# The first 512 rows: weights of three blocks per transfer, ScalarE's copy ahead of the next root, the next tile's turn between up products

## The chip, the cores and the metric

The kernel runs on one core of one Trainium2 chip. The metric is the device time of one execution in microseconds (us), the median over several runs. The engines of the core work side by side, each through its own list of instructions in order: TensorE (PE) multiplies matrices, VectorE (DVE) and ScalarE (ACT) do elementwise work, GpSimd (POOL) helps, and SyncE (SP) issues most of the transfers from the large memory. They wait for each other through semaphores.

## What is computed

The input x has 2048 rows of 640 columns. It is normalised row by row, and the result xn goes through two parts: an attention part of 32 heads (keys and values of the last 512 positions), and a gated part with weights of 640 x 1536. The two are multiplied at the end.

```python
def _B_ref(x, w_gate, w_up, w_down):
    g = jnp.einsum("bsd,df->bsf", x, w_gate)
    u = jnp.einsum("bsd,df->bsf", x, w_up)
    h = _sigmoid(g) * u
    return jnp.einsum("bsf,fd->bsd", h, w_down)

x = A_x
xn = _layernorm(x, axis=-1)
s = _A_ref(xn, A_k_cache, A_v_cache, A_wq, A_wo)
g = _silu(_B_ref(xn, B_w_gate, B_w_up, B_w_down))
return x + s * g
```

The change lies in the first two products of `_B_ref` and in the normalisation, for the first 512 rows alone.

## The kernel before

The 2048 rows are four groups of 512, and a group is four tiles of 128 rows. The 1536 columns of `w_gate` and `w_up` are 12 blocks of 128, the 640 columns of x five chunks of 128. For a group, the loop over the blocks (`for f in range(NF)`) makes ten matmuls per block, five chunks for the gate and five for the up product, each 128 x 128 weights against 512 rows (L487). ACT takes the sigmoid of the gate (L492), DVE multiplies it with the up product into `hT_sb` (L493). The results of a block lie in two banks of PSUM, and four such pairs (`bank2`) are used in turn.

These matmuls need xn turned, so that its columns lie on the partitions. Groups 1 to 3 are turned by a transposing transfer. Group 0 has nothing to hide behind, so its tiles are handled one by one, in the order written out in the loop `for q in range(TQ)`, and the first three blocks (FA = 3) are multiplied tile by tile as each becomes ready:

- `ln_part`, `ln_stats` (L357, L362): DVE's statistics of a tile, in two parts of 320 columns, and their sum.
- `ln_sqrt` (L401): ACT's square root. The reciprocal (L418) and `ln_apply` (L372) on DVE give the tile of xn; that of tile 0 comes in two pieces.
- `turn` (L408): PE transposes the five chunks of the tile into one of two PSUM banks, and ACT copies them (L410) into `xnT[0]`, which stands as `mid` in the profile.
- `first_mm(q, f)` (L395): ten matmuls of 128 x 128 weights against the 128 rows of tile q, the five chunks of the gate and then the five of the up product of block f.
- `warm_up` (L385): products of zeros that keep PE busy, nine ahead of everything and two behind the turn of tile 0.

In this order a tile is turned one or two blocks ahead of the products that use it. Tile 1 is turned behind block 0 of tile 0, and block 1 of tile 0 comes behind it; block 2 of tiles 0 and 1 is put off until tile 2 is turned, block 2 of tile 2 until tile 3 is turned. On ACT the root of tile q + 1 stands ahead of the copy of tile q.

All loads of the first rows are issued from SP's queue in the written order: x tiles 0 and 1, then gate and up weights in pieces given by `f_cuts` (three pieces of one block, then three of three blocks), with x tiles 2 and 3 behind the first two pairs of pieces, and the x of group 1 behind the fourth pair. `load_w` (L330) issues one piece, `load_x` (L309) one tile of x, `load_x4` (L314) four. From the ninth transfer on, an issue also waits for the landing of the one eight places ahead of it. Behind the weights follow four loads of `wq` for a scan (L201).

Of the kernel before, what the change touches and what calls it, by code (L numbers as in the profile page):

```python
# [17 lines left out]
def kernel(  # L18
# [14 lines left out]
    P = 128  # L33
# [7 lines left out]
    F = B_w_gate.shape[1]  # L41
# [8 lines left out]
    TQ = 4  # L50
    NCD = D // P
# [4 lines left out]
    G = 2  # L56
    NG = NPAIR // G
    assert NG == 8 and HQDH == 48 * P and NST == 4
    NWARM = (9, 2)
    FA = 3  # L60
    PC = 3
    GC = 2 * G * DH
# [212 lines left out]
    with ExitStack() as bctx:  # L275
# [31 lines left out]
        def load_x(t):  # L307
            x_sb = xin_pool.tile([P, D], BF16, name=f"x_sb{t}")
            nc.sync.dma_start(x_sb[:], xf[t * P:(t + 1) * P, :])  # L309
            x_tiles[t] = x_sb[:]  # L310

        def load_x4(s):
            x_sb = xin_pool.tile([P, TQ, D], BF16, name="x_sb4")
            nc.sync.dma_start(  # L314
                x_sb[:], xf[s * 512:(s + 1) * 512, :].rearrange("(q p) d -> p q d", p=P)
            )
            for q in range(TQ):
                x_tiles[s * TQ + q] = x_sb[:, q, :]

        wg_sb = wB.tile([P, NCD, F], BF16, name="wg_sb")  # L320
        wu_sb = wB.tile([P, NCD, F], BF16, name="wu_sb")
        wg_r = B_w_gate.rearrange("(c p) f -> p c f", p=P)
        wu_r = B_w_up.rearrange("(c p) f -> p c f", p=P)
        f_cuts = [0, P, 2 * P, 3 * P, 6 * P]
        while f_cuts[-1] < F:
            f_cuts.append(min(F, f_cuts[-1] + 3 * P))

        def load_w(w_sb, w_r, k):
            f = slice(f_cuts[k], f_cuts[k + 1])
            nc.sync.dma_start(w_sb[:, :, f], w_r[:, :, f])  # L330
# [3 lines left out]
        for k in range(len(f_cuts) - 1):  # L334
            load_w(wg_sb, wg_r, k)
            load_w(wu_sb, wu_r, k)
            if k < 2:
                load_x(2 + k)
            elif k == 3:
                load_x4(1)  # L340
        wd_sb = wB.tile([P, NF, D], BF16, name="wd_sb")
        for i in range(4):
# [11 lines left out]
        def ln_part(t, i):  # L354
            if i == 0:
                stats_t[t] = bwork.tile([P, nsub, nc.vector.BN_STATS_DIM], F32, name="stats")
            nc.vector.bn_stats(stats_t[t][:, i, :], x_tiles[t][:, i * fsz:(i + 1) * fsz])  # L357

        def ln_stats(t, i0=0):
            for i in range(i0, nsub):  # L360
                ln_part(t, i)
            nc.vector.bn_aggr(mv[:, t, :], stats_t[t][:])  # L362
# [5 lines left out]
        def ln_apply(t):  # L368
            xn = xpool.tile([P, D], BF16, name="xn")
            cuts = [0, 2 * P, D] if t == 0 else [0, D]  # L370
            for d in map(slice, cuts, cuts[1:]):
                nc.vector.tensor_scalar(  # L372
                    xn[:, d], x_tiles[t][:, d], mv[:, t, 0:1], rstd[:, t, :],
                    op0=ALU.subtract, op1=ALU.mult,
                )
            return xn
# [6 lines left out]
        def warm_up(n):  # L383
            for _ in range(n):
                nc.tensor.matmul(w_ps, lhsT=warm[:, 0:P], rhs=warm[:], start=True, stop=True)  # L385

        warm_up(NWARM[0])

        gu_first = [bank2() for _ in range(FA)]

        def first_mm(q, f):
            r = slice(q * P, (q + 1) * P)
            for i, w in enumerate((wg_sb, wu_sb)):
                for c in range(NCD):
                    nc.tensor.matmul(  # L395
                        gu_first[f][:, i, r], lhsT=w[:, c, f * P:(f + 1) * P], rhs=xnT[0][:, c, r],
                        start=(c == 0), stop=(c == NCD - 1),
                    )

        def ln_sqrt(q):  # L400
            nc.scalar.activation(  # L401
                rstd[:, q:q + 1, :], mv[:, q:q + 1, 1:2], AF.Sqrt, bias=eps_t[:], scale=1.0
            )

        def turn(q):
            pT = pT_banks[:, q % 2, 0:NCD * P // 2].bitcast(BF16).rearrange("p (c n) -> p c n", c=NCD)
            for c in range(NCD):
                nc.tensor.transpose(pT[:, c, :], xn_t[q][:, c * P:(c + 1) * P], ident[:])  # L408
            for cs in ((slice(0, 2), slice(2, NCD)) if q == 0 else (slice(0, NCD),)):
                nc.scalar.activation(xnT[0][:, cs, q * P:(q + 1) * P], pT[:, cs, :], AF.Copy)  # L410

        xn_t = {}
        ln_stats(0)
        ln_sqrt(0)
        for q in range(TQ):
            if q + 1 < TQ:
                ln_part(q + 1, 0)
            nc.vector.reciprocal(rstd[:, q:q + 1, :], rstd[:, q:q + 1, :])  # L418
            xn_t[q] = ln_apply(q)
            if q + 1 < TQ:  # L420
                ln_stats(q + 1, 1)
                ln_sqrt(q + 1)
            if q == 0:
                turn(0)
                warm_up(NWARM[1])
                continue
            first_mm(q - 1, 0)
            turn(q)
            first_mm(q - 1, 1)
            if q == 2:  # L430
                first_mm(0, 2)
                first_mm(1, 2)
            elif q == 3:
                first_mm(2, 2)
        for f in range(FA):
            first_mm(TQ - 1, f)

        def ln_rest(t):
            xn = ln_apply(t)
# [483 lines left out]
    for r, (pi, g) in enumerate(runs):  # L923
# [23 lines left out]
        for k, (q, x) in enumerate(pv_list):  # L947
# [5 lines left out]
            if pi == 0 and 1 <= g < 5 and k == 6:  # L953
                w = wo_in[3 * g % 4]
# [260 lines left out]
```

## Time and profile before

| | us |
|---|---|
| median of 3 runs | 872.84 (872.71 to 873.98) |
| the profiled execution, whole | 873.17 |
| its span, first to last instruction | 871.4 |
| PE busy | 864.6 |
| DVE busy | 674.6 |
| ACT busy | 625.5 |
| POOL busy | 212.4 |

The span is that of one profiled execution; its whole time has 1.8 us more, around the span. The first rows end where the loop of L487 begins, near 15 us. In the timeline a row has its start, the time from the first start to the last end of the instructions merged in it, engine, line, operation, output <- inputs, how many there are, and in square brackets how long the engine stood idle before it and what released it. The end of a matmul is modelled: back to back, matmuls of 128 columns start every 0.056 us, but each is shown as 0.22 us long. In the chain of waits a row has a start, a length and what ran; "issue" is time in which nothing shown was waited for. A row of transfers has the form, how many, KB, and the median time from issue to landing.

### The profile page before, as it was taken

To read this page: it belongs to the slowest core of one execution; us is meant where nothing else is said; L and a number is where in the kernel's file an instruction comes from. 1 tells how busy PE (TensorE), PEld (TensorE's weight loads), DVE (VectorE), ACT (ScalarE), POOL (GpSimd) and SP (SyncE) were. 2 spreads that over 40 slices of the span, in tenths; PEclk is the share of its full clock that TensorE was granted. 3 is DMA by queue.
4 is the path that set the end of the run, shared out by engine and by line. 5 is a ranking of instruction groups with operands and counts; after the bars stand their busy time and mean duration, and the time that the engine had idled before them with its cause. 6 is when DMAs were issued, how large, how long until landed. Compare 5 with 4: busy or idle time off the path is not lost.

```text
span 871.4 us, 18973 instructions
## 1 busy us (share of the span) xinstructions
PE 864.6 (99%) x7558; PEld 565.2 (65%) x7569; DVE 674.6 (77%) x1137; ACT 625.5 (72%) x772; POOL 212.4 (24%) x299
## 2 busy tenths in 40 slices
PE   8999999999999999999999999999999999999998
PEld 5444455756766756756756756756777777777776
DVE  6587777777777777777677777787878587989997
ACT  6868676488888788788788787774655667666662
POOL 0000239406406406406406406300000111000000
PEclk9999999999999999999999999999999999999999
DMA  9999982699699799699689779497788788465841
GB/s 273 273 273 223 269 178 56 88 240 197 136 251 195 153 235 190 146 246 183 153 223 170 165 180 215 111 293 203 202 208 231 249 277 279 146 226 203 283 161 38
DMA packets 264712, 174.69 MB, mean 200 GB/s; under 512 B 162256, under 2 KB 249680, under 8 KB 264624
## 3 DMA queue, kind: packets, MB, share of 16 engines
q1 hardware_dynamic: 258192, 153.23, 69.3%
q0 software_dynamic: 6432, 20.26, 11.6%
q8 instruction: 59, 0.97, 0.5%
q14 instruction: 29, 0.24, 0.1%
HBM read 102.11 MB, written 35.13 MB: 157 GB/s over the span
## 4 chain that ended last, share of the span: by engine, by line
PE 96%; DVE 2%; ACT 1%; issue 1%; DMA 0%; ACTq 0%; DVEq 0%
PE ps_all L1022 24%; PE ps_all L606 21%; PE ps_all L714 20%; PE ps_all L700 19%; PE ps_all L487 9%; PE ps_all L560 1%; PE ps_all L395 1%; ACT sig_sb L492 1%; ACT mid L244 0%; DVE stats L357 0%; DVE arm L1006 0%; DMA x_sb<-in_A_x_dram 0%; DVE hT_sb L493 0%; DVE arm L1077 0%; DVE arm L1075 0%
## 5 line engine op out<-in xcount | busy, mean ns | idle before, releaser
L704 ACT ACTIVATE E<-ps_all 128x1024 bf16<-128x1024 f32 x256 | 251.2, 1022 | 113.5 <-PE ps_all L700 112.8
L700 PE MATMUL ps_all<-qT,kT 64*128 64x512 bf16 x1536 | 198.2, 376 | 0.0
L714 PEld LDWEIGHTS <-E 128*128 128x128 bf16 x2048 | 169.7, 98 | 8.1 <-issue 8.1
L714 PE MATMUL ps_all<-v_sb,E 128*128 128x193 bf16 x2048 | 174.0, 247 | 0.0
L644 DVE TENSOR_TENSOR qT<-ps_all,qp 128x512 bf16<-128x512 f32 x174 | 115.5, 687 | 47.4 <-PE ps_all L606 38.6
L1022 PEld LDWEIGHTS <-mid 128*128 128x128 f16 x1176 | 115.0, 98 | 44.6
L700 PEld LDWEIGHTS <-kT 64*128 64x128 bf16 x1536 | 84.4, 94 | 80.1 <-issue 4.4
L627 DVE COPY qp<-ps_all 128x512 f32<-128x512 f32 x150 | 100.5, 687 | 46.3 <-PE ps_all L606 46.3
L721 DVE TENSOR_TENSOR o_st<-ps_all,rden 128x768 bf16<-128x768 f32 x128 | 122.5, 957 | 4.4
L606 PE MATMUL ps_all<-mid 64*128 64x512 f16 (+1 forms) x840 | 105.9, 376 | 0.0
L606 PE MATMUL ps_all<-mid,arm 64*128 64x512 f16 (+1 forms) x840 | 105.5, 376 | 0.0
L606 PEld LDWEIGHTS <-mid 64*128 64x128 f16 x840 | 48.0, 94 | 44.2 <-issue 0.7
L606 PEld LDWEIGHTS <-arm 64*128 64x128 f16 x840 | 47.0, 94 | 44.7 <-issue 0.2
L1022 PE MATMUL ps_all<-arm,mid 128*128 128x320 f16 x462 | 67.5, 299 | 0.0
L835 ACT ACTIVATE mid<-mid,w_sc 128x1536 f16<-128x1536 bf16 (+1 forms) x41 | 60.2, 1493 | 0.3 <-DMA mid<-oT_d 0.3
L244 ACT ACTIVATE mid<-mid,w_sc 128x1536 f16<-128x1536 bf16 x37 | 58.2, 1573 | 2.2 <-DVE w_sc L222 1.6
L1022 PE MATMUL ps_all<-op,mid 128*128 128x320 f16 x378 | 55.1, 299 | 0.0
L493 DVE TENSOR_TENSOR hT_sb<-ps_all,sig_sb 128x512 bf16<-128x512 f32 x48 | 32.7, 684 | 26.4 <-ACT sig_sb L492 16.0
L230 POOL DMA_DIRECT2D mid<-in_A_wq_dram x74 | 43.9, 598 | 22.0 <-DVE mid L266 21.9
L1022 PE MATMUL ps_all<-mid 128*128 128x320 f16 x336 | 48.2, 299 | 0.0
L262 POOL TENSOR_TENSOR arm<-mid 128x384 f16<-128x384 f16 x20 | 18.1, 904 | 114.7 <-ACT mid L244 113.6
L720 DVE RECIPROCAL rden<-ps_all 128x4 f32<-128x4 f32 x128 | 23.3, 182 | 27.9 <-PE ps_all L714 26.3
(185 smaller groups left out, 1057.0 us busy)
## 6 DMA issues: line engine op xcount, KB each, us to landing
oT_d<-oT SPq DMA_DIRECT2D x64, 384.0 KB, 5.4
mid<-oT_d SPq DMA_DIRECT2D x46, 384.0 KB, 4.9
mid<-in_A_wq_dram POOLq DMA_DIRECT2D x74, 192.0 KB, 6.3
mid<-in_A_wq_dram SPq DMA_DIRECT2D x16, 480.0 KB, 7.7
arm<-in_A_wo_dram SPq DMA_DIRECT2D x16, 480.0 KB, 5.6
v_sb<-in_A_v_cache_dram SPq DMA_DIRECT2D x32, 192.0 KB, 5.8
kraw<-in_A_k_cache_dram SPq DMA_DIRECT2D x28, 192.0 KB, 3.7
h_d<-hT_sb SPq DMA_DIRECT2D x12, 384.0 KB, 7.3
```

The costliest lines, as they stand in the source:

```text
L230: eng.dma_start(raw[r], wq_r[:, c, :, g * GC:(g + 1) * GC])
L244: nc.scalar.activation(raw.bitcast(F16), raw, AF.Copy, scale=w_up)
L487: nc.tensor.matmul(gu[:, i, :], lhsT=w[:, c, f * P:(f + 1) * P], rhs=xnT[s][:, c, :], start=(c == 0), stop=(c == NCD - 1),)
L606: nc.tensor.matmul(ps_all[:, b, :], lhsT=w(r, c), rhs=x[r, c, :], start=(first and k == 0), stop=(k == len(cs) - 1), skip_group_check=True,)
L627: nc.vector.tensor_copy(dst, part(b))
L644: nc.vector.tensor_tensor(q_out(i, u, pp), part(b), t, ALU.add)
L700: nc.tensor.matmul(ps[:, b, :], lhsT=kT[h, c * PC + j, :], rhs=qT_t[r][i, j][h, pp, :], start=(j == 0), stop=(j == PC - 1),)
L704: nc.scalar.activation(E_t[r, i, pp][:, c, :, :], ps, AF.Exp, scale=scale_qk)
L714: nc.tensor.matmul(o_ps[:, q // 2, q % 2, 0:DH + 1], lhsT=E[:, c, h, q * P:(q + 1) * P], rhs=vt[:, c, 0:DH + 1], start=(c == 0), stop=(c = ...
L721: nc.vector.tensor_tensor(o_st[:, :, h * DH:(h + 1) * DH].rearrange("p (b i) d -> p b i d", b=2), o_ps[:, :, :, 0:DH], rden[:].to_broadcas ...
L835: eng.activation(t, t.bitcast(BF16), AF.Copy, scale=up)
L1022: nc.tensor.matmul(ps_all[:, b, d0:d1], lhsT=a[:, c, :], rhs=w[:, c, d0:d1], start=(start and c == 0), stop=(c == nk - 1), skip_group_chec ...
```

## The change

`f_cuts` becomes four pieces of three blocks each, so the first six loads of weights (160 KB each) are two of 480 KB, and x tiles 2 and 3 are issued behind these two. `first_mm` takes the gate (0) or up (1) product and a list of blocks. A tile is turned ahead of the last up product of the tile before it. ACT copies every tile in two halves, and the statistics' last part and the root of the next tile come behind the copy. Where the first part of the next tile's statistics stands ahead of the reciprocal (q = 0 and 2), it stays there; for q = 1 both parts come behind. One warm-up product is taken out.

```diff
-    NWARM = (9, 2)
+    NWARM = (9, 1)
...
-        f_cuts = [0, P, 2 * P, 3 * P, 6 * P]
-        while f_cuts[-1] < F:
-            f_cuts.append(min(F, f_cuts[-1] + 3 * P))
+        f_cuts = list(range(0, F + 1, FA * P))
...
             load_w(wu_sb, wu_r, k)
-            if k < 2:
-                load_x(2 + k)
-            elif k == 3:
+            if k == 0:
+                load_x(2)
+                load_x(3)
+            elif k == 1:
                 load_x4(1)
...
-        def first_mm(q, f):
+        def first_mm(q, i, *fs):
             r = slice(q * P, (q + 1) * P)
-            for i, w in enumerate((wg_sb, wu_sb)):
+            w = (wg_sb, wu_sb)[i]
+            for f in fs:
                 for c in range(NCD):
...
-            for cs in ((slice(0, 2), slice(2, NCD)) if q == 0 else (slice(0, NCD),)):
+            for cs in (slice(0, 2), slice(2, NCD)):
                 nc.scalar.activation(xnT[0][:, cs, q * P:(q + 1) * P], pT[:, cs, :], AF.Copy)
...
         for q in range(TQ):
-            if q + 1 < TQ:
+            early = q in (0, 2)
+            if early:
                 ln_part(q + 1, 0)
             nc.vector.reciprocal(rstd[:, q:q + 1, :], rstd[:, q:q + 1, :])
             xn_t[q] = ln_apply(q)
+            if q > 0:
+                first_mm(q - 1, 0, 0, 1, 2)
+                first_mm(q - 1, 1, 0, 1)
+            turn(q)
+            if q == 0:
+                warm_up(NWARM[1])
+            else:
+                first_mm(q - 1, 1, 2)
             if q + 1 < TQ:
-                ln_stats(q + 1, 1)
+                ln_stats(q + 1, int(early))
                 ln_sqrt(q + 1)
-            if q == 0:
-                turn(0)
-                warm_up(NWARM[1])
-                continue
-            first_mm(q - 1, 0)
-            turn(q)
-            first_mm(q - 1, 1)
-            if q == 2:
-                first_mm(0, 2)
-                first_mm(1, 2)
-            elif q == 3:
-                first_mm(2, 2)
-        for f in range(FA):
-            first_mm(TQ - 1, f)
+        first_mm(TQ - 1, 0, 0, 1, 2)
+        first_mm(TQ - 1, 1, 0, 1, 2)
```

## The prediction

> **What bounds the kernel now.** The page's slices and chain come first: TensorE (PE) is busy nearly everywhere, at the full granted clock, and makes 96% of the chain that ended last.
>
> ```profile
> PE   8999999999999999999999999999999999999998
> PEclk9999999999999999999999999999999999999999
> PE 96%; DVE 2%; ACT 1%; issue 1%; DMA 0%; ACTq 0%; DVEq 0%
> ```
>
> The change touches only the first 26 us. There I read the chain of waits in order of time. It is a ladder of loads, VectorE (DVE) and ScalarE (ACT) steps up to 8.74 us, and from there it runs on PE alone.
>
> ```profile
> 7.76 0.29 ACT rstd L401
> 8.06 0.64 ACT mid L410
> 8.74 0.72 PE ps_all L395 x10
> 9.51 0.45 PE ps_all L408 x5
> 9.96 2.23 PE ps_all L395 x40
> 12.19 0.28 PE ps_all L408 x5
> 12.47 2.79 PE ps_all L395 x50
> ```
>
> A small matmul takes 2.23/40 = 0.0558 us of PE. The first rows need 120 products (L395) and, behind tile 0, 15 transposes (L408): 135 x 0.0558 = 7.53 us. In the timeline the first product starts at 6.68 and the last group of five at 14.82, so PE is free for L487 at 14.82 + 5 x 0.0558 = 15.10. Of these 8.42 us only 0.89 are idle.
>
> ```profile
> 5.62 0.59 PE L385 MATMUL ps_all<-warm 128*128 128x512 bf16 x2
> 6.07 0.29 ACT L401 ACTIVATE rstd<-mv,eps_t 128x1 f32<-128x1 f32 x1 [1.54 <-DVE mv L362]
> 6.27 0.74 ACT L410 ACTIVATE mid<-ps_all 128x256 bf16<-128x256 bf16 x2
> 6.68 0.71 PE L395 MATMUL ps_all<-mid,wg_sb 128*128 128x128 bf16 x5 [0.47 <-ACT mid L410]
> 7.51 0.44 PE L408 MATMUL ps_all<-ident,xn 128*128 128x128 bf16 x5
> 7.99 0.70 ACT L410 ACTIVATE mid<-ps_all 128x640 bf16<-128x640 bf16 x1
> 8.74 0.44 PE L395 MATMUL ps_all<-mid,wg_sb 128*128 128x128 bf16 x5 [0.23 <-ACT mid L410]
> 14.82 0.44 PE L395 MATMUL ps_all<-mid,wu_sb 128*128 128x128 bf16 x5
> ```
>
> The reader is to see three things. ACT's copy of tile 0 begins at 6.27, behind the root of tile 1 (6.07), although the transposes ended at 5.79. Behind every later turn PE has work that does not need that turn's copy: 10 products at 7.79, 30 at 9.79, 20 at 12.31. And a copy in two halves lets PE in after the first half (6.27 to 6.68), but PE then stands again: its first group takes 0.71 instead of 0.44, because chunk 2 waits for the second half and starts at 7.07.
>
> **Part 1, the copy ahead of the next root.** The last transpose of tile 0 still ends at 5.79, and tile 1's turn shows that a free ACT copies 0.04 later (7.51 + 0.44 to 7.99). So the halves start at 5.83. By tile 0's row the first product follows 0.41 after the start of the copies and chunk 2 follows 0.79 after it: 6.24 and 6.62. Gain at the start 0.44. One warm-up product fewer is worth nothing: with one, PE would be free at about 5.84, and the copies hold it till 6.24. The root of tile 1 moves to about 6.48 (ACT starts an instruction 0.1 before the last one ends), and the reciprocal and normalisation behind it (0.15, 0.45) end at 7.44 instead of 7.08. Reciprocal and normalisation of tiles 2 and 3 wait the same way behind the copies of tiles 1 and 2.
>
> **Part 2, the turn between up products.** Per tile the order is now 15 gate products, 10 up products, the turn, the last 5 up products, and then the next tile's gates, which need the copy just begun. Let T be the start of a turn. PE issues the turn and five products until T + 0.56. The transposes end at T + 0.44, the copies start at T + 0.48, the first product follows at T + 0.89 and chunk 2 at T + 1.27. Between lie two products (0.11), so PE idles 0.33 + 0.27 = 0.60 per turn. Before, it idled 0.24 behind tile 1 and nothing behind tiles 2 and 3: those 30 and 20 products were the cover, and this order removes it. In the program's list of instructions only the first half carries a wait for PE, so I take it that it waits for all five transposes; if it needed two only, the gap would be about 0.44.
>
> Splitting the copy is costed from tile 0: both halves 0.74 together against 0.70 whole. Bounds: 0 extra, or nothing overlapping, which a root of one column (0.29, nearly all fixed cost) puts at +0.29. I take the pair's own row. By the Trainium skill (ScalarE: Activation LUTs, Rules for kernel authors), an activation costs about 0.3 us plus a price per element; two halves would then cost 0.3 more than one copy, and the sum below would be about 1 us worse. The pair in this trace does not agree.
>
> **The sum.** First product 6.24; chunk 2 at 6.62. Then 13 gates and 10 ups: T1 = 6.62 + 23 x 0.0558 = 7.91. Chunk 2 of tile 1 at 9.18, T2 = 10.46, T3 = 13.02, chunk 2 of tile 3 at 14.29, and 28 products more: 15.86. Before 15.10: **0.76 us later**.
>
> The turns do not wait for DVE: tile 1 is ready at 7.44 against T1 = 7.91; tiles 2 and 3, whose roots start when the copies end (T + 1.22) and take 0.86 with reciprocal and normalisation, are ready at 10.00 and 12.55 against 10.46 and 13.02. That cover is about 0.4; beyond it, each tenth that a root is late is a tenth on the path.
>
> **Part 3, the loads.** SP's queue issues two loads of 480 KB where it had six of 160 KB, and x2 and x3 go behind both. All later loads move four places up the queue. The bytes per block do not change.
>
> ```profile
> wg_sb<-in_B_w_gate_dram SPq DMA_DIRECT2D x1, 160.0 KB, 3.0
> wu_sb<-in_B_w_up_dram SPq DMA_DIRECT2D x1, 160.0 KB, 3.4
> wg_sb<-in_B_w_gate_dram SPq DMA_DIRECT2D x1, 480.0 KB, 5.6
> wu_sb<-in_B_w_up_dram SPq DMA_DIRECT2D x1, 480.0 KB, 5.9
> 8.41 0.49 DVE L357 BATCH_NORM_STATS2 stats<-x_sb 128x6 f32<-128x320 bf16 x1 [0.68 <-DMA x_sb<-in_A_x_dram]
> ```
>
> These are times from issue to landing, for issues at 1.66, 2.13, 5.99 and 7.06. The second x tile lands at 3.5. The first 480 KB load landed 2.1 after the load ahead of it (wu of block 2 at 9.5, wg at 11.6), the next 1.4 later. So the three gate blocks land at about 5.6 (needed at 6.2), the up blocks at 7.0 (needed at 7.35, after 15 gates), x2 at 7.5 and x3 at 8.0 (x3 before: 8.4). Bounds for the up blocks: 3.5 + 2 x 1.4 = 6.3, and with the slowest interval of this queue, 2.4 for 480 KB (blocks 6 to 8: gate at 16.5, up at 18.9), 8.3. So the price is 0 to 0.95; I take 0, since 7.0 is the nearest pair. DVE uses x2 from 7.5, 0.1 after it is free, and x3 about 8.6; both have the root of tile 2 (9.04) as cover. Nothing is gained by earlier landings, since PE asks for nothing sooner.
>
> **What follows.** L487 runs on PE without a gap, so a later start moves all of it. ACT's last copy ends at about 14.25 instead of 13.21, so table load (1.28) and sigmoids are 1.04 late, 0.28 worse than PE. PE writes four buffers in turn, so that is four blocks (2.16 each) away from holding it. I expect the shift to reach the end whole: 871.4 + 0.76 = 872.2 of span, with the 1.8 around it 873.9 for the profiled run. That run (873.17) was 0.33 above the median shown, so for the median **872.84 + 0.76 = 873.6**.
>
> **Rivals.** (a) *The up weights come late.* For it: 480 KB in one piece holds all three blocks back, and one interval was 2.4. Against: the nearest pair fits. Cost 0.35 (both intervals 2.1) to 0.95: 873.9 to 874.6, say 874.2.
>
> (b) *Not slower: the second half hides.* Place: PE behind each turn. If the products did not stand for the second half, the gap would be 0.33, the start would have none, and L487 would start at 6.24 + 7.53 + 3 x 0.33 = 14.76: 0.34 earlier, 872.5. It decides below a gap of 0.35 per turn (6.24 + 0.27 + 7.53 + 3 x 0.35 = 15.10). For it: a free ACT and an early start of 0.44. Against: the 0.71 group at 6.68. Even with no gap at all the gain would be 1.33, 871.5.
>
> (c) *The halves do not overlap:* 0.25 to 0.29 more at four places, about +1.0 on the sum, 874.6. For it: the long fixed part of a root. Against: the pair's 0.74. The ScalarE rule of the Trainium skill named above speaks for this one.
>
> (d) *The shift is lost on the way*, at a wait that does not follow PE: 872.8. For it: PE waits 0.15 for DVE at 115.63. Against: that chain starts from PE at 98.37 and would move with it.
>
> **How the numbers follow.** Forecast 0.62, (a) 0.16, (b) 0.11, (c) 0.07, (d) 0.04. The runs before lie from 872.71 to 873.98, so 0.2% (1.75 us) is about what a measurement of this kernel can tell from no change. Forecast, (b) and (d) are all within it, (a) mostly; the upper ends of (a) and (c) reach it. Faster by that much is beyond even a ladder without gaps and needs scatter. So faster 0.04, same 0.82, slower 0.14. Range: from (b) at 872.5, a little less for scatter, to past (c) at 874.6: 872.3 to 874.9.
>
> **What would show it.** Right: the copies of tile 0 near 5.83, the first product near 6.24; three times PE idle near 0.3 twice behind a turn, put down to the copies (L410); the last L395 product ending near 16.0. Wrong: PE waiting for wu before 8 us (a), groups of five after a turn that take 0.44 throughout (b), a pair of halves near 1.0 (c), or an end of L487 that has not moved with its start (d). If PE stands for xn at a turn, the 0.4 of cover failed.

## The result, and the profile after

| | before | changed |
|---|---|---|
| median, us | 872.97 (11 runs, 872.71 to 873.98) | 875.10 (11 runs, 874.70 to 875.73) |
| span of the profiled execution | 871.4 | 873.3 |
| PE busy | 864.6 | 865.8 |
| first matmul of the loop of 12 blocks | 15.10 | 16.39 |

The changed kernel is slower: ratio 1.0024, 95% interval 1.0015 to 1.0033, 2.13 us between the medians. 0.76 was forecast, and 875.1 lies 0.2 above the range.

The page of the changed kernel, slices and chain:

```profile
PE   8999999999999999999999999999999999999998
PEclk9999999999999999999999999999999999999999
PE 89%; DVE 3%; DMA 3%; ACT 3%; issue 1%; SPq 0%; DVEq 0%; ACTq 0%
```

PE is as busy as before and its clock is full. The chain leaves PE for other engines at two places: in the first rows, and between 38 and 117 us, where PE, ACT, DVE and the transfers run within tenths of each other and the chain follows whichever came last. PE itself lost little there: its longest stand is 0.35, near 62 us.

The chain of waits, in order of time (start, length, what ran):

```profile
2.14 5.63 DMA wu_sb<-in_B_w_up_dram
7.76 0.05 issue
7.81 0.73 PE ps_all L395 x10
8.54 0.29 PE ps_all L408 x5
8.84 0.02 issue
8.86 0.77 ACT mid L410 x2
9.63 0.04 issue
9.67 1.44 PE ps_all L395 x23
11.12 0.29 PE ps_all L408 x5
11.41 0.02 issue
11.43 0.77 ACT mid L410 x2
12.21 0.04 issue
12.25 1.44 PE ps_all L395 x23
```

Before, the first 8.7 us of this chain were statistics and roots, and behind them it was PE alone. Now it is one load until 7.76, that of three blocks of up weights, and behind it PE and the copies (L410) in turn: three copies of 0.77 lie on the path (the third at 14.01). The timeline has the same in PE's and DVE's waits:

```profile
5.79 0.77 ACT L410 ACTIVATE mid<-ps_all 128x256 bf16<-128x256 bf16 x2 [1.31 <-PE ps_all L408]
6.33 1.16 PE L395 MATMUL ps_all<-mid,wg_sb 128*128 128x128 bf16 x15 [0.36 <-DMA wg_sb<-in_B_w_gate_dram]
7.81 0.73 PE L395 MATMUL ps_all<-mid,wu_sb 128*128 128x128 bf16 x10 [0.32 <-DMA wu_sb<-in_B_w_up_dram]
8.21 0.89 DVE L356 BATCH_NORM_STATS2 stats<-x_sb 128x6 f32<-128x320 bf16 x2 [0.80 <-DMA x_sb<-in_A_x_dram]
9.29 1.27 PE L395 MATMUL ps_all<-mid,wg_sb 128*128 128x128 bf16 x15 [0.19 <-ACT mid L410]
11.87 1.27 PE L395 MATMUL ps_all<-mid,wg_sb 128*128 128x128 bf16 x15 [0.19 <-ACT mid L410]
```

Fifteen matmuls without a gap take 1.00 here (14 starts of 0.056 and one length of 0.22); the groups behind a turn take 1.27, with 0.27 of waiting for the second half of the copy inside. The idle times in brackets count from the modelled end of the last matmul, 0.16 behind the point at which the next could have started. By starts, as in the text below, PE stood 0.35 where a row has 0.19, and 0.48 where it has 0.32. The transfers from issue to landing, for issues at 1.67, 2.14, 2.71 and 3.27:

```profile
wg_sb<-in_B_w_gate_dram SPq DMA_DIRECT2D x1, 480.0 KB, 4.6
wu_sb<-in_B_w_up_dram SPq DMA_DIRECT2D x1, 480.0 KB, 5.6
x_sb<-in_A_x_dram SPq DMA_DIRECT2D x1, 160.0 KB, 5.5
x_sb<-in_A_x_dram SPq DMA_DIRECT2D x1, 160.0 KB, 5.4
```

The gate weights land at 6.3, the up weights at 7.76, x2 at 8.2 and x3 at 8.7. Forecast were 5.6, 7.0, 7.5 and 8.0.

**Where the time went by stage.** The table is taken from the starts of the first matmuls of the stages in the traces (a stage that begins with a missing record counts from the last product before it): the start of the 12-block loop, its length, the down projection (L560 before), attention from there to the output part, the output part (L1022 before), and from the start of the last matmul to the end. Both kernels were traced twice.

| trace | start | 12 blocks | down | attention | output | end | span |
|---|---|---|---|---|---|---|---|
| before | 15.10 | 97.12 | 13.57 | 524.76 | 216.75 | 4.09 | 871.4 |
| before, second | 15.38 | 97.40 | 13.18 | 524.76 | 216.75 | 4.10 | 871.6 |
| changed | 16.39 | 97.47 | 13.40 | 524.75 | 216.95 | 4.36 | 873.3 |
| changed, second | 16.48 | 97.34 | 13.17 | 526.78 | 216.95 | 4.35 | 875.1 |

Three columns differ between the kernels in both traces: the start (+1.29 in the first pair, +1.10 in the second), the output part (+0.20) and the end (+0.26). The two middle columns trade a few tenths with each other in either kernel. The 2.03 in the attention of the second trace is one execution's; no other trace of this study has it.

### The profile page after: what moved, and what is told of

It reads as the page before. It is cut to its first block, busy times and chain, and to the rows that moved or that the text cites. A ratio compares the mean times of both kernels' runs of the same rounds, so it can differ in the third digit from the quotient of the medians.

```text
span 873.3 us, 18979 instructions
## 1 busy us (share of the span) xinstructions
PE 865.8 (99%) x7568; PEld 565.2 (65%) x7568; DVE 675.1 (77%) x1137; ACT 625.5 (72%) x775; POOL 212.3 (24%) x299
## 4 chain that ended last, share of the span: by engine, by line
PE 89%; DVE 3%; DMA 3%; ACT 3%; issue 1%; SPq 0%; DVEq 0%; ACTq 0%
PE ps_all L1019 24%; PE ps_all L603 21%; PE ps_all L711 20%; PE ps_all L697 19%; PE ps_all L484 2%; DMA mid<-in_A_wq_dram 2%; PE ps_all L557 1%; DVE hT_sb L490 1%; ACT sig_sb L489 1%; ACT mid L300 1%; DMA wu_sb<-in_B_w_up_dram 1%; PE ps_all L395 1%; DMA h_d<-hT_sb 1%; ACT mid L244 1%; DVE stats L356 0%
```

## The experiments

Times are medians, beside those of the kernel before in the same sessions (872.95 to 873.16). "Start" is the start of the 12-block loop.

**The changed order of products with the loads of before.**

```diff
-        f_cuts = list(range(0, F + 1, FA * P))
+        f_cuts = [0, P, 2 * P, 3 * P, 6 * P]
...
-            if k == 0:
-                load_x(2)
-                load_x(3)
-            elif k == 1:
+            if k < 2:
+                load_x(2 + k)
+            elif k == 3:
```

> The changed kernel with the loads of before put back (six weight loads of 160 KB, x2 and x3 between them). Theory (the new order of the products needs the whole of three blocks early, so order and loads hang together): the gate of block 2 can't start before its load lands (9.05 before), the 15 gates of tile 0 end near 9.4, and the rest follows as in the changed kernel: first L487-type product at about 17.9 (15.10 before, 16.39 in the changed kernel), time about 875.8. Rival (only the gaps behind the turns cost, the loads are hidden): 15.9 and 873.7.

875.99 us, ratio 1.0039 (1.0025 to 1.0053), start 17.72. PE's row in the timeline of this kernel:

```profile
8.87 0.45 PE L396 MATMUL ps_all<-mid,wg_sb 128*128 128x128 bf16 x5 [1.56 <-DMA wg_sb<-in_B_w_gate_dram]
```

Ten gate products ran at 6.25, and those of block 2 stood for their load until 8.87. The order of the products needs the new loads: undoing the loads alone is worse than the change.

**The kernel before with the new loads.** The same lines of the diff, the other way.

> The kernel before with the loads of the change alone (three blocks in one transfer, x2 and x3 behind them). Theory (late x2 and up weights are a cost of their own): the up product of block 0 waits till 7.8, and x2, landing near 8.1, holds the statistics that stand ahead of tile 1's reciprocal, so tile 1 is turned near 9.4; from there no gaps; loop of 12 blocks starts near 17.2, time near 875.1. Rival (the loads cost only the wait for the up weights): start near 15.7, time 873.6.

875.80 us, ratio 1.0030 (1.0019 to 1.0041), start 17.63. Tile 1 was turned at 9.15, near the 9.4 of the theory, since x2 landed near 8.05 and its statistics stand ahead of tile 1's reciprocal. The theory had no gaps behind that, and there were none; yet the start was 0.4 later than expected. Two stretches of the trace, and two rows of PE in the second, show a cost that the theory did not have (length, busy time and count of PE, its weight loads, DVE, ACT and POOL, then the granted clock, DMA share and GB/s):

```profile
5.50:8.91 3.41, 1.75 (x16) 0.88 (x14) 1.26 (x5) 0.95 (x3) 0.00 (x0) 1.00 1.08 345
8.91:12.33 3.42, 3.18 (x31) 3.19 (x32) 2.91 (x10) 1.18 (x3) 0.00 (x0) 0.50 1.09 347
9.66 0.74 PE L394 MATMUL ps_all<-mid,wg_sb 128*128 128x128 bf16 x5
10.19 0.74 PE L394 MATMUL ps_all<-mid,wu_sb 128*128 128x128 bf16 x5
```

The second stretch ran at half the granted clock. Its products stood 0.11 apart instead of 0.056, so that the 30 starts from 9.15 to 12.32 took 3.17 where 1.67 would have done. At the full clock part of that would have been waiting for the copy of tile 1, which ended at 10.65. The start missed the expectation by 0.4 only, so the expected 17.2 was itself too late. The seven runs fall into two groups: three with a mean granted clock of 0.999 or 1.0 took 874.60 to 874.82, four with 0.997 or 0.998, the traced one among them, 875.80 to 876.74. At the full clock the new loads alone cost about 1.7; the median has the clock in it.

**Each tile turned behind the gates, ahead of all 15 up products.**

```diff
                 first_mm(q - 1, 0, 0, 1, 2)
-                first_mm(q - 1, 1, 0, 1)
             turn(q)
...
-                first_mm(q - 1, 1, 2)
+                first_mm(q - 1, 1, 0, 1, 2)
```

> The changed kernel, but each tile is turned ahead of all 15 up products instead of the last 5, so that 10 more products lie over the copy. Theory (the gap of 0.6 behind each turn is missing cover): no gap over 0.1 behind the turns; PE stands instead for the up weights till 7.8 and for tile 2 near 10.4 (x2 is late); the loop of 12 blocks starts near 15.4 instead of 16.39, time near 874.1. Rival (PE stands for the copies wherever the turn is, or the lateness of tile 2 and 3 on VectorE takes it all back): start within 0.2 of 16.39, time 875.1.

874.31 us, ratio 1.0014 (1.0005 to 1.0024), start 15.57. PE in the timeline:

```profile
7.91 1.01 PE L395 MATMUL ps_all<-mid,wu_sb 128*128 128x128 bf16 x15
8.76 1.00 PE L395 MATMUL ps_all<-mid,wg_sb 128*128 128x128 bf16 x15
10.53 0.45 PE L408 MATMUL ps_all<-ident,xn 128*128 128x128 bf16 x5 [0.77 <-DVE xn L371]
10.82 1.00 PE L395 MATMUL ps_all<-mid,wu_sb 128*128 128x128 bf16 x15
11.66 1.06 PE L395 MATMUL ps_all<-mid,wg_sb 128*128 128x128 bf16 x15
```

The gates behind a turn take 1.00 and 1.06 instead of 1.27, with no wait ahead of them: the gaps were missing cover. 0.82 of the start came back. Of the 1.86 of three gaps, 0.93 was spent again ahead of the turn of tile 2, whose x had landed late.

**Six loads of 160 KB, in the same order of bytes** (three gate blocks, three up blocks, x2, x3).

```diff
+        for w_sb, w_r in ((wg_sb, wg_r), (wu_sb, wu_r)):
+            for k in range(FA):
+                load_w(w_sb, w_r, k)
+        load_x(2)
+        load_x(3)
```

> The changed kernel with the same order of bytes, but the two loads of 480 KB cut into six of 160 KB (three gate blocks, three up blocks, x2, x3). Theory (products wait for the landing of a whole transfer of three blocks): the up product of block 0 is not held any more (its load lands near 6.6), start of the loop of 12 blocks near 15.9 instead of 16.39, time near 874.6. Rival (the bytes set it; packets of 256 B are slower, x2 comes later still): start 16.4 to 16.8, time 875.1 to 875.5.

874.93 us, ratio 1.0021 (1.0011 to 1.0030), start 16.68: the rival. Up products began at 7.45, but the next blocks followed in pieces (gaps of 0.24 and 0.09), and tile 2 was 0.40 late at its turn. Smaller landings helped one wait, and the bytes, in smaller packets, gave it back: x2, behind the same bytes as in the changed kernel, landed at 9.02 instead of 8.19.

**Gate weights in place of the up weights in the first 512 rows**, and the up weights of three blocks loaded behind x2 and x3. This leaves out the real up products of the three blocks.

```diff
         load_w(wg_sb, wg_r, 0)
         load_x(2)
         load_x(3)
         load_w(wu_sb, wu_r, 0)
...
-            w = (wg_sb, wu_sb)[i]
+            w = wg_sb
```

> The changed kernel with the up weights of the first three blocks loaded behind x2 and x3, and with gate weights in their place in the first 512 rows (this leaves out the real up products of three blocks there): nothing waits for up weights and x2 comes early. Theory (gaps behind the turns and late up weights are separate terms, 0.76 and 0.4): the first 15 gates and the up products follow without a wait, the gaps of 0.33 and 0.27 stay, start of the loop near 15.9 to 16.0, time near 874.6. Rival (the wait for the up weights lay over something else that is late, as tile 1 or 2): start within 0.1 of 16.39.

874.73 us, ratio 1.0018 (1.0009 to 1.0027), start 16.06.

```profile
6.65 1.57 PE L396 MATMUL ps_all<-mid,wg_sb 128*128 128x128 bf16 x25 [0.70 <-DMA wg_sb<-in_B_w_gate_dram]
8.05 0.44 PE L409 MATMUL ps_all<-ident,xn 128*128 128x128 bf16 x5
8.33 0.44 PE L396 MATMUL ps_all<-mid,wg_sb 128*128 128x128 bf16 x5
8.97 1.83 PE L396 MATMUL ps_all<-mid,wg_sb 128*128 128x128 bf16 x25 [0.19 <-ACT mid L411]
```

Without the up weights 25 products run through, and the start comes 0.33 earlier, although the gate weights landed 0.3 later than in the changed kernel. From the first product to the start it is 9.41 instead of 10.06, a difference of 0.65: 0.48 for the wait for up weights in the changed kernel, 0.16 for the second half of tile 0's copy, which had ended here. The gaps behind the turns stay. The two terms are separate.

**Four tiny loads more, in the changed kernel and in the kernel before.** The following lines were added to each, behind the loads of the weights:

```diff
+        for i in range(4):
+            more = bone.tile([P, 16], BF16, name=f"more{i}")
+            nc.sync.dma_start(more[:], xf[i * P:(i + 1) * P, 0:16])
```

> The changed kernel with four tiny loads (128 rows of 32 bytes, read by nobody) behind its weights, so that SP's queue issues as many transfers as before. Theory (the change issues four transfers fewer, which shifts every later transfer to another of the eight completion counters that are used in turn; at the end SP looks at the counters in a fixed order, and four more looks then stand behind the last store): start of the loop of 12 blocks unchanged near 16.4, from the start of the last matmul to the end of the span 4.09 us as before instead of 4.36, the late stall of 0.19 near 700 us gone too; span 872.8 to 872.9 and, if the 0.35 stall near 62 us goes by the same cause, 872.5. Rival (the end and the stalls belong to the later start or are scatter): 4.36 and a span of 873.3.

> The kernel before with the same four tiny loads behind its weights: the same shift of the counters with the first rows untouched. Theory: start of the loop at 15.10 as before, 4.34 from the last matmul to the end instead of 4.09, span 871.65, or 871.85 with the stall near 700 us. Rival: 4.09 and a span of 871.4.

| trace | start | 12 blocks | output | end | time |
|---|---|---|---|---|---|
| changed | 16.39 | 97.47 | 216.95 | 4.36 | 875.10 |
| changed, four more | 16.71 | 97.47 | 216.95 | 4.10 | 875.28 |
| before | 15.10 | 97.12 | 216.75 | 4.09 | 872.97 |
| before, four more | 15.23 | 98.20 | 216.75 | 4.33 | 873.19 |

The end moved as the theory said, in both directions, with the number of transfers alone. The 0.20 of the output part and the stall in the 12 blocks did not follow it: that half of the theory fell. The 98.20 of the last row is that of the slowest of its eleven runs (874.32), the one that was traced. In the times nothing shows: ratio 1.0029 (1.0019 to 1.0038) and 1.0003 (0.9994 to 1.0012). A quarter of a microsecond is below what they tell, and the start of the first was 0.3 later, because its gate weights landed 0.3 later in that trace.

**Two scan loads less on SP's queue** (pieces 10 and 11 of 16 are left out).

```diff
+        if i in (10, 11):
+            return
         eng.dma_start(scan_t[i], wq_n[:, :, i * NSC:(i + 1) * NSC])
```

> The changed kernel without the scan loads 10 and 11 of wq, 480 KB each, which stand on SP's queue just ahead of the transposing transfers of group 2 (two of 16 pieces of the scan are left out). Theory (the stall of 0.35 near 62 us is the last of these transposing transfers, queued behind a backlog of bytes): it lands 1.5 to 2.9 earlier against PE, no stall there, and the down projection starts 0.35 earlier against the start of the loop of 12 blocks. With two transfers fewer again the counters move by two, so the end grows from 4.36 to about 4.46 to 4.5. Span 872.9 to 873.1, time 874.8. Rival (the transfers wait for VectorE's tiles, not for bytes): stall of 0.3 or more stays.

874.63 us, ratio 1.0019 (1.0009 to 1.0028). The last transposing transfer of group 2 landed at 58.8 (62.0 in the changed kernel, where PE wanted it at 61.7), the 12 blocks took 97.12, and the end grew to 4.47, all by the theory.

**Second traces of both kernels.**

> The changed kernel unchanged, for a second trace. Theory (gaps, late up weights, the stall near 62 us, the late 0.20 and the end belong to the program): all five are there again, landings within 0.3 us. Rival (one of them is scatter of one execution): it is missing or differs by more than half.

> The kernel before unchanged, for a second trace. Theory: start of the loop within 0.1 of 15.10, no stall near 60 us, last stage 216.75 and end 4.09. Rival (scatter): one of these differs by 0.2 or more.

876.86 and 873.36, one run each; the rows stand in the table by stage. Gaps, late weights, output part and end of the changed kernel came again. The stall near 60 us did too (0.2 of it), but the kernel before had one of 0.28 there in its second trace. So it is not the change's. For the kernel before the rival held: its start came at 15.38, 0.28 later than in its first trace, and 0.21 of it was a wait for the up weights of block 1. The start read from one trace is good to about 0.3.

**The copies ahead of the roots alone**, in the kernel before, with its loads, its products and whole copies for tiles 1 to 3; block 1 of tile 1 goes ahead of the turn of tile 2.

```diff
-            if q + 1 < TQ:
-                ln_stats(q + 1, 1)
-                ln_sqrt(q + 1)
...
+            if q == 2:
+                first_mm(1, 1)
             turn(q)
+            if q + 1 < TQ:
+                ln_stats(q + 1, 1)
+                ln_sqrt(q + 1)
```

> The kernel before with its own loads, products and whole copies, but each copy ahead of the next tile's root on ScalarE, and block 1 of tile 1 ahead of the turn of tile 2 (its root is later). Theory (this part gains 0.44 at the first product, and gives most of it back because roots and so tiles 1 and 2 come later): first product 6.24, loop of 12 blocks from 14.9 to 15.0 instead of 15.10, time 872.8, no difference that can be measured. Rival (the gain at the start is kept): start 14.66, time 872.5.

873.07 us, ratio 1.0000 (0.9991 to 1.0009). The first product ran at 6.21 and the start was 15.04: 0.48 gained at the first product, 0.06 left at the start.

```profile
7.45 0.45 PE L408 MATMUL ps_all<-ident,xn 128*128 128x128 bf16 x5 [0.26 <-DVE xn L372]
```

Ahead of this turn PE stood 0.42 for tile 1, whose root is later, as the theory said. Another 0.23 went to the up weights of block 1, a wait that the second trace of the kernel before has too. No version here beats the kernel before.

## Why the prediction was wrong, point by point

**Sign and main term.** The sign of the sum was right, though by the prediction's own mark of 1.75 us the 2.13 count as slower, to which it gave 0.14. The largest term, the gaps behind the turns, was right in place and size: 0.60 per turn forecast, 0.35 + 0.27 = 0.62 measured three times. Turning at the gates took them away. One reading was off without touching the sum: before, PE stood 0.40 behind the turn of tile 1 by starts (8.29 to 8.74, less one product), not 0.24, and 0.21 more ahead of the turn of tile 2.

**The copy ahead of the root.** Copies at 5.83 and the first product at 6.24 were forecast, 5.79 and 6.33 measured; the 0.09 more are the gate weights. The two halves took 0.77 together, not 0.74, so rival (c), halves that don't overlap, did not happen.

**The step that failed: "the price is 0 to 0.95; I take 0, since 7.0 is the nearest pair".** The up weights landed at 7.76, so that PE stood 0.48 between gate and up products (0.58 in the second trace). This is rival (a), to which I gave 0.16. In five other traces with these loads the up weights landed at 7.59 to 8.09, never near 7.0. The lateness is the gate load's: it landed 2.7 behind the second x tile (3.57 to 6.28), where 2.1 was taken, and the up load followed 1.5 later, where 1.4 was taken. The pair that I took as nearest landed on a queue already in flow. Here the flow fell to nearly nothing at the change to packets of 768 bytes. The transfers' row of the changed kernel from 2.1 to 6.1 us has 40 slices of 0.1 us, and behind it stands that of the kernel before from 7.0 to 11.0:

```profile
GB/s 166 294 410 359 333 307 282 384 254 164 143 46 46 23 92 138 230 230 230 223 223 292 300 284 353 369 353 353 346 346 361 346 346 369 346 369 369 353 369 364
GB/s 282 251 228 271 269 289 297 277 277 241 256 256 248 233 172 128 156 205 192 133 161 192 177 253 300 323 338 330 361 361 369 369 330 330 346 338 361 369 369 353
```

In the changed kernel the slices fall from 3.0 on to 23 and recover to 138 at 3.6, until 4.1 they stay at 230 or less, and only from 4.5 on do they have 346 and more. The trace of before had shown a shallower dip at its own first loads of three blocks (128 to 205 GB/s from 8.4 to 9.3), and I did not look there. That the deeper dip is what made the gate load late is argued from these rows; no experiment removes it. Why the first packets are slow stays open.

The start of the first trace adds up: forecast 15.86, gate weights +0.09, less of the first tile's half copy left to wait for -0.11, up weights +0.48, gaps +0.06, together 16.38 against 16.39 measured.

**The second step that failed: "I expect the shift to reach the end whole".** It did, but 0.46 came on top that the sum had no term for. The end grew by 0.26. The four transfers fewer I had priced by their landings only. In the traces every transfer of SP's queue reports to one of eight completion counters (semaphores), used in turn. At the end SP waits for the counters in a fixed order, one pair every 0.06 us. Four transfers fewer put the last store on an earlier counter of that order, and four more waits then stand behind its landing, from 872.24 to 872.45 in the changed kernel. Three kernels showed it: 4.10 with the count restored, 4.33 with it shifted in the kernel before, 4.47 with two fewer again. All thirteen traces follow the count: 4.08 to 4.11 with 456 transfers on SP's queue, 4.33 to 4.36 with 452 or 460, 4.47 with 450.

The output part is 0.20 longer, by a stall near 700 us, where the timelines of the changed kernel and of the kernel before have these rows:

```profile
700.62 0.44 ACT L1026 ACTIVATE u2s<-ps_all 128x320 f32<-128x320 f32 x1 [0.70 <-DVE mid L834]
698.89 0.44 ACT L1029 ACTIVATE u2s<-ps_all 128x320 f32<-128x320 f32 x1 [0.43 <-PE ps_all L1022]
```

216.95 was measured in both traces of the change and in four variants with the new loads and a new order of products; 216.75 in all the others. The releaser in the first row is inferred. ACT's last wait for semaphores ahead of that row ended at 700.30, and the row starts 0.32 later; in all six traces with 216.95 it is 0.32, in the seven others 0.04 or 0.05. What ACT stood for in that time is not shown. The 0.20 does not follow the number of transfers. Its cause was not found.

**The sum against the time.** Start 1.10 to 1.29, output part 0.20, end 0.26: 1.6 to 1.75. The medians differ by 2.13. The remaining 0.4 to 0.6 is not placed; a single trace differs by that much in the middle stages. For the first pair of traces the columns add up to the 1.92 by which the spans differ, with 0.35 more in the 12 blocks and 0.17 less in the down projection; but the traced run of the kernel before lay 0.20 above its median.

**Rivals (b) and (d).** (b) fell with the groups of 1.27. (d) is not shown: the down projection took 13.57 in the first trace of the kernel before, where PE came earliest, and 13.17 to 13.40 in the changed kernel, but 13.18 in the second trace of the kernel before too.

**The cover of 0.4 on DVE** held in the changed kernel: no turn waited for xn, though x2 came 0.7 later than forecast. With the turn moved ahead it failed at once (0.77 at tile 2).

## What to carry to other kernels

A turn needs as much independent work behind it as its copy takes, here 1.3 us from the first transpose to the last chunk; moving it later in the same work gains nothing and opens a gap per tile. Merging loads makes the first user wait for the last byte of the merged piece: a landing priced from a queue in flow came out 0.7 to 0.8 too early here for the first transfers of a queue, so a plan that needs them should have that much room. Where a microsecond counts, look at the number of transfers too, for a store that falls on another completion counter can cost a quarter of one at the end.

## What the runs showed of the hardware

The granted clock of PE fell to half for 3.41 us in the kernel before with the new loads, behind a stretch of 3.41 us in which PE was still busy for 1.75. The Trainium skill (TensorE: Matmul & The Clock Gate, Part 1) puts the fall behind an idle window of about 3.4 us. The length agrees, the idleness doesn't: half-idle was enough here. Counted in the same steps of 3.41 us from the time at which the clock became full, a stretch from 4.38 to 7.80 with 2.56 busy in the changed kernel kept the full clock, and so did one from 7.54 to 10.95 with 1.86 busy in the changed kernel with the loads of before. That is a risk of gaps which the prediction had not counted. The changed kernel did not show it in its two traces, nor in the mean clock of its eleven runs (0.999 or 1.0); with the four tiny loads one run of ten has 0.997, and it is the slowest (878.61).

ACT's second half copy costs almost nothing: 0.77 for both halves against 0.70 for a whole tile. The Trainium skill (ScalarE: Activation LUTs, Rules for kernel authors) budgets about 0.3 us for an activation whose bias is a pointer operand, besides a price per element. The root, which has such a bias (`eps_t`), agrees with 0.29. The copies have none, so the prediction and its rival (c) used that rule where it does not hold; for a second copy queued behind the first, the traces show 0.07.
